# Output weights in two transfers, and sixteen partitions of the last w_down rows loaded halfway through

## The chip, the cores and the metric

The kernel runs on one core of one Trainium2 chip. The metric is the device time of one launch in microseconds; smaller is better. Times named "at 397.69" are counted from the first instruction of the profiled execution.

## The reference

One decoding step of a transformer block with one new token: a pre-norm attention over a long cache, then a pre-norm gated feed-forward part. All tensors are bf16.

```
h  = x + attention(layernorm(x)) @ wo
h2 = h + (gelu(layernorm(h) @ w_gate) * (layernorm(h) @ w_up)) @ w_down
```

x has 1024 elements (D). There are 32 query heads and 4 key/value heads of 128 elements, so 8 query heads share one key/value head. The cache holds 65536 positions: K and V are 64 MB each. wq and wo have 8 MB each (1024 x 4096 and 4096 x 1024), w_gate and w_up 7 MB each (1024 x 3584), w_down 7 MB (3584 x 1024). Every byte is read once, 173 MB in all.

## The kernel before

Everything is built around one stream of loads, issued by SP in the order of use: wq, then K and V in turns, then wo, w_gate, w_up, w_down. The loads go to `ring`, four slots of 4 MB (32 KB in each of 128 partitions). Slots 0 and 1 (keys R0, R1) take V, slots 2 and 3 (R2, R3) take K; afterwards wo has slots 2 and 3, w_gate 0 and 1, w_up 2 and 3, and w_down 0 and 1 again. The last four rows per partition of w_down do not fit and have a place of their own, `w_end` (128 partitions x 4 rows x 1024, 1 MB), into which nothing else is ever loaded.

Attention runs in eight stages `t` (4 key/value heads x 2 halves of the cache), about 38.7 us each. In a stage, VectorE transposes K in four chunks, TensorE makes the scores (`pe_loop`, a hardware loop), VectorE finds a maximum, ScalarE computes the exponentials (`softmax`, eight activations, keys `lp<t>_<r>`), TensorE multiplies them with V into `acc`, and ScalarE copies `acc` out (`acc_copy`). For every stage SP issues one V load and two K loads. A K half waits until the scores that used its slot are done (semaphore `s_qk`, one step per score group, 32 in all); a V load waits until the stage before has finished with V (`s_step`).

The instructions of an engine stand in the order in which the program is written, through a small recorder (`Flow`): `op` and `dma` note each operation with the keys that it reads and writes, and `issue` sends them out with the waits that follow from the keys. `f.dma(engine, ...)` issues a transfer on that engine's queue (SP's and ACT's are used); each transfer adds 16 to a semaphore when it has landed.

wo is one transfer of 8 MB into both slots; it waits for all 32 score groups (`done`). TensorE then multiplies the attention output with it in 64 matmuls, adds x, and the second norm follows. w_gate, w_up and w_down come by one large transfer each, and w_down in four pieces: 16 rows per partition (`wa`, 4 MB, slot 0), 8 rows (`w_body`, 2 MB, slot 1), then the four rows of `w_end` in two transfers of three rows and one row, with semaphores of their own (`end_sem`). These last two are not recorded by `Flow` but written behind it.

The end is written out by hand: four matmuls that keep TensorE awake (`stay_busy`), a wait for `wa`, 32 wide matmuls (`down_wide`), a copy of their sums by ScalarE (`e_sb`), `add_wide`, a wait for `w_body`, 64 small matmuls (`down`), a wait for each of the `w_end` transfers with 24 and 8 matmuls, two casts, and the output transfer of four partitions.

The profile puts nearly all recorded operations down to one line (L105, in `issue`). Lines of their own have the loop (L436 to L471), the `w_end` transfers (L612), and at the end `down` (L621), `stay_busy` (L628), `down_wide` (L636), `add_wide` (L642) and the copy to `e_sb` (L652).

## Time and profile before

| what | value |
|---|---|
| time, median of 3 runs | 409.34 us (409.29 to 409.46) |
| profiled execution, its own time | 409.97 us |
| its span, first to last instruction | 408.3 us |
| TensorE busy, weight loads aside | 226.1 us (55%) |
| VectorE busy | 201.0 us (49%) |
| ScalarE busy | 40.0 us (10%) |
| bytes read from HBM | 173.02 MB, 424 GB/s over the span |
| mean granted TensorE clock | 0.807 |

The profile is of one execution. Its strip cuts the span into 40 equal slices; a digit is a busy share in tenths, 9 for 90% or more. In the list of DMA queues, q1 is SP's and q10 ACT's; q8 and q14 fetch instructions. In the timeline, a row has the start, the time that its instructions take together, engine, line, operation, and in brackets how long the engine was idle before and who released it; PEq is TensorE's own sequencer. In the table of windows, the columns are the window, its length, busy time and number of instructions of PE, PEld, DVE, ACT and POOL, the granted clock, the busy share of the 16 DMA engines and GB/s.

### The profile page before, as it was taken

The numbers are of one execution on the slowest core, as the hardware profiler recorded it, in microseconds if no ns is written. First come the engines' busy times: TensorE is split into PE (matmuls) and PEld (weight loads), VectorE is DVE, ScalarE is ACT, GpSimd is POOL, SyncE is SP. The second block draws the span as 40 slices with busy tenths as digits, with TensorE's granted clock in tenths as the row PEclk, the third lists the DMA queues.
The fourth block names the chain that finished last, engine by engine and source line by source line (L and its number), as shares of the span: only waits on it lengthen the run. The fifth ranks groups of instructions, "written<-read, shape, count | busy, mean of one in ns | idle before, by whom it ended". The sixth has DMA issues, their size and how long they took to land. (4 is left out here: it accounts for less than half of the span.)

```text
span 408.3 us, 3718 instructions
## 1 busy us (share of the span) xinstructions
PE 226.1 (55%) x1557; PEld 100.1 (25%) x1558; DVE 201.0 (49%) x160; ACT 40.0 (10%) x142; POOL 16.6 (4%) x27
## 2 busy tenths in 40 slices
PE   0433855574677468715863685467456746344156
PEld 0111312231232133202321232233132213132122
DVE  2228760894089328734961686089407940121010
ACT  1000003001300120030003000300130013000000
POOL 4210000001000000010000001000000000020000
PEclk9975995899569778978896689589976986686688
DMA  8999999999999999999999999999999999999994
GB/s 360 411 446 425 459 414 424 446 417 444 424 456 424 411 450 462 417 411 427 485 417 411 417 469 405 424 449 424 443 417 462 417 417 469 405 440 445 401 419 193
DMA packets 4814, 173.10 MB, mean 424 GB/s; under 512 B 580, under 2 KB 584, under 8 KB 840
## 3 DMA queue, kind: packets, MB, share of 16 engines
q1 hardware_dynamic: 4760, 173.02, 98.4%
q8 instruction: 4, 0.07, 0.1%
q14 instruction: 2, 0.02, 0.0%
q10 hardware_dynamic: 48, 0.00, 0.0%
HBM read 173.02 MB, written 0.00 MB: 424 GB/s over the span
## 5 line engine op out<-in xcount | busy, mean ns | idle before, releaser
L105 DVE STREAM_TRANSPOSE ktb<-ring 128x4096 f32<-128x4096 f32 x32 | 141.1, 4418 | 74.3 <-DMA ring<-in_A_k_cache_dram 74.3
L450 PE MATMUL bank<-ktb,qs 128*128 128x512 bf16 x512 | 131.7, 416 | 54.4 <-PEq L436 54.4
L450 PEld LDWEIGHTS bank<-ktb,qs 128*128 128x128 bf16 x512 | 51.4, 103 | 131.5 <-issue 85.6
L462 PE MATMUL bank<-ring,pt 128*32 128x512 bf16 x512 | 43.9, 518 | 36.5 <-PEq L436 36.5
L105 ACT ACTIVATE pt<-sc,nb 128x256 bf16<-128x256 f32 x64 | 31.5, 493 | 258.3 <-DVE nb L105 258.3
L105 DVE STREAM_TRANSPOSE sc<-bank 128x512 f32<-128x512 f32 x32 | 22.2, 695 | 38.0 <-PE bank L450 38.0
L462 PEld LDWEIGHTS bank<-ring,pt 128*32 128x32 bf16 x512 | 18.6, 125 | 58.7 <-issue 54.4
L105 PE MATMUL bank<-ring,xz 128*32 128x512 bf16 (+1 forms) x192 | 16.0, 505 | 21.7 <-DMA ring<-in_B_w_up_dram 7.7
L105 DVE STREAM_TRANSPOSE ktb<-bank 128x512 f32<-128x512 f32 (+1 forms) x6 | 4.0, 672 | 32.9 <-PE bank L105 32.6
L105 DVE TENSOR_REDUCE mx<-sc 128x8 f32<-128x2048 f32 x8 | 18.3, 2286 | 0.3
L454 PE MATMUL bank<-ident_f,mx 128*8 128x128 f32 x8 | 2.6, 320 | 25.8 <-PEq L436 25.8
L105 POOL COPY qs<-qsel 128x512 bf16<-128x512 bf16 x4 | 5.3, 1326 | 233.5 <-PE bank L450 219.5
L105 PEld LDWEIGHTS bank<-ring,xz 128*32 128x32 bf16 x192 | 6.4, 125 | 30.0 <-issue 15.6
L105 ACT ACTIVATION_READ_ACCUMULATOR pt<-sc,nb 128x1 f32 x64 | 11.9, 186 | 0.0
L471 PE MATMUL bank<-sel,acc_sb 128*128 128x8 f32 x64 | 8.2, 255 | 6.2 <-PEq L436 6.2
L471 PEld LDWEIGHTS bank<-sel,acc_sb 128*128 128x128 f32 x64 | 7.7, 191 | 10.0 <-issue 10.0
L105 ACT COPY acc_sb<-bank 128x512 f32<-128x512 f32 x8 | 4.7, 586 | 46.5 <-PE bank L462 46.5
L454 PEld LDWEIGHTS bank<-ident_f,mx 128*8 128x8 f32 x8 | 0.7, 83 | 29.5 <-issue 29.5
L105 PE MATMUL bank<-ring,ktb 128*32 128x512 bf16 x64 | 5.2, 492 | 4.7 <-DMA ring<-in_A_wo_dram 4.7
L456 PE MATMUL bank<-diag,ones_f 8*128 8x8 f32 x16 | 3.7, 299 | 5.7 <-PEq L436 5.7
L105 POOL MEMSET ktb<- 128x1024 bf16 (+2 forms) x3 | 3.5, 1164 | 76.6 <-PE bank L450 76.6
L105 DVE TENSOR_TENSOR h_col<-bank,x_col 128x8 f32<-128x8 f32 x1 | 0.2, 166 | 12.3 <-PE bank L105 12.3
(97 smaller groups left out, 60.9 us busy)
## 6 DMA issues: line engine op xcount, KB each, us to landing
ring<-in_A_k_cache_dram SPq DMA_DIRECT2D x16, 4096.0 KB, 25.1
ring<-in_A_wq_dram SPq DMA_DIRECT2D x2, 4096.0 KB, 16.6
ring<-in_B_w_gate_dram SPq DMA_DIRECT2D x1, 7168.0 KB, 26.1
ring<-in_B_w_up_dram SPq DMA_DIRECT2D x1, 7168.0 KB, 28.9
ring<-in_B_w_down_dram SPq DMA_DIRECT2D x1, 4096.0 KB, 22.0
ring<-in_B_w_down_dram SPq DMA_DIRECT2D x1, 2048.0 KB, 26.5
w_end<-in_B_w_down_dram SPq DMA_DIRECT2D x1, 768.0 KB, 27.7
w_end<-in_B_w_down_dram SPq DMA_DIRECT2D x1, 256.0 KB, 10.5
```

The source lines that it names most:

```text
L105: ins = getattr(self.eng[e], o["call"])(**o["kw"])
L450: m = nc.tensor.matmul(bank[c][:], lhsT=qs[:, jt].rearrange("p s c -> p (s c)")[:, s * P:(s + 1) * P], rhs=mv[:, :, J, :, u], start=(s == ...
L454: nc.tensor.transpose(out=mxT_ps, in_=mx1[:], identity=ident_f[:]).then_inc(s_step, 1)
L456: nc.tensor.matmul(bc_ps, lhsT=ones_f[0:rep, :], rhs=diag[:], start=True, stop=True).then_inc(s_step, 1)
L462: m = nc.tensor.matmul(acc[32 * q:32 * q + 32, :], lhsT=pt[:, c, n, :, :].rearrange("p h s -> p (h s)"), rhs=v_sb[:, c, :, n, :], start=(c ...
L471: m = nc.tensor.matmul(o_ps, lhsT=acc_sb[:, u * Dh:(u + 1) * Dh], rhs=sel[:, u:SQ:NS], start=(u == 0), stop=(u == NS - 1))
```

## The change

There are two parts.

First, wo comes in two transfers of 4 MB, by heads 0 to 15 and 16 to 31 of each partition's rows. The first goes into slot 2 and waits for 30 of the 32 score groups, those that read slot 2; the second goes into slot 3 and waits for all 32. The matmuls read the key of their own half.

Second, the four `w_end` rows of the last 16 partitions (112 to 127) are loaded by five transfers of 5, 4, 3, 2 and 2 partitions, issued on ACT's queue behind `acc_copy(3)`, which is half way through the eight stages. Each moves 8 KB per partition. They share the semaphore of the load of x. The two `w_end` transfers at the end now move 112 partitions. TensorE waits for the five early transfers together with `w_body`, ahead of the 64 matmuls of `down`. In the order of SP's instructions, the first `w_end` transfer now stands behind the barrier at the end of the recorded part, where it stood ahead of it.

```diff
+    x_sem = tc.alloc_semaphore("x_landed")
...
+    FA = CW // D
+    FB = FC - FA
+    wb_src = B_w_down[P * FA:F, :].rearrange("(p e) n -> p e n", p=P)
+    early = [5, 4, 3, 2, 2]
+    PE0 = P - sum(early)
+
+    def early_rows():
+        p0 = PE0
+        for n in early:
+            at = f.dma("act", w_end[p0:p0 + n, :, :], wb_src[p0:p0 + n, FB - FZ:FB, :], r=["lp3_0"], sem=x_sem)
+            p0 += n
+        return at
...
         if t + 1 < NT2:
             acc_copy(t)
+        if t == 3:
+            early_at = early_rows()
...
-    f.dma("sp", wv, A_wo.rearrange("(p c) n -> p c n", p=P), w=["R2", "R3"], wait=done, sem=r_sem[2])
+    wo_v = A_wo.rearrange("(p c) n -> p c n", p=P)
+    HC = Hq // 2
+    f.dma("sp", wv[:, 0:HC, :], wo_v[:, 0:HC, :], w=["R2"], wait=[(s_qk, NT2 * CPH - DCH)], sem=r_sem[1])
+    f.dma("sp", wv[:, HC:Hq, :], wo_v[:, HC:Hq, :], w=["R3"], wait=done, sem=r_sem[2])
...
-            op("pe", "matmul", r=["o2z", "R2", "R3"], w=["B6"], ...
+            op("pe", "matmul", r=["o2z", "R%d" % (2 + c // HC)], w=["B6"], ...
...
-        d = nc.sync.dma_start(out=w_end[:, e1 - FB + FZ:e2 - FB + FZ, :], in_=wb_src[:, e1:e2, :])
+        d = nc.sync.dma_start(out=w_end[0:PE0, e1 - FB + FZ:e2 - FB + FZ, :], in_=wb_src[0:PE0, e1:e2, :])
...
+        nc.tensor.wait_ge(x_sem, early_at)
         nc.tensor.wait_ge(sem2, at2)
```

More of the change, by code (lines that the diff above doesn't have):

```diff
@@ L220 @@
     x_in = sb("x_in", [XU, XV, DC], BF16)
+    x_sem = tc.alloc_semaphore("x_landed")
     ones_f = sb("ones_f", [P, P])
     op("dve", "memset", w=["ones_f"], ap=ones_f[:], constant=1.0)
-    f.dma("act", x_in[:], A_x[0, 0].rearrange("(u v j) -> u v j", u=XU, j=DC), w=["x_in"], r=["ones_f"], sem=tc.alloc_semaphore("x_landed"))
+    f.dma("act", x_in[:], A_x[0, 0].rearrange("(u v j) -> u v j", u=XU, j=DC), w=["x_in"], r=["ones_f"], sem=x_sem)
     wq_tiles = []
@@ L415, in acc_copy @@
         op("act", "copy", wait=[(s_step, STEPS * t + 4)], inc=(from_act, 1), out=acc_sb[:], in_=acc[:])
+    FA = CW // D
[3 more added lines that the diff above has]
+    PE0 = P - sum(early)
+    assert PE0 % 16 == 0
+    def early_rows():
[4 more added lines that the diff above has]
+        return at
     for t in range(NT2):
@@ L519 @@
     op("pool", "tensor_copy", r=["o2_bf"], w=["o2z"], out=o2z[:, :, 0], in_=o2_bf[:])
-    FA = CW // D
-    FB = FC - FA
     at_ps = bank[6][:]
     wv = slot(2, 2).rearrange("p (c n) -> p c n", c=Hq)
-    f.dma("sp", wv, A_wo.rearrange("(p c) n -> p c n", p=P), w=["R2", "R3"], wait=done, sem=r_sem[2])
+    wo_v = A_wo.rearrange("(p c) n -> p c n", p=P)
+    HC = Hq // 2
+    f.dma("sp", wv[:, 0:HC, :], wo_v[:, 0:HC, :], w=["R2"], wait=[(s_qk, NT2 * CPH - DCH)], sem=r_sem[1])
+    f.dma("sp", wv[:, HC:Hq, :], wo_v[:, HC:Hq, :], w=["R3"], wait=done, sem=r_sem[2])
     for c in range(Hq):
@@ L529 @@
             q = 2 * (c % 2) + s
-            op("pe", "matmul", r=["o2z", "R2", "R3"], w=["B6"], out=at_ps[32 * q:32 * q + 32, :], lhsT=o2z[:, c, :],
+            op("pe", "matmul", r=["o2z", "R%d" % (2 + c // HC)], w=["B6"], out=at_ps[32 * q:32 * q + 32, :], lhsT=o2z[:, c, :],
                rhs=wv[:, c, :].rearrange("k (p s c) -> k s p c", s=DS, c=C4)[:, s], start=(c < 2), stop=(c >= Hq - 2), tile_position=(0, 32 * q))
@@ L600 @@
     wb = slot(1)[:, 0:FB * D].rearrange("p (e n) -> p e n", e=FB)
-    wb_src = B_w_down[P * FA:F, :].rearrange("(p e) n -> p e n", p=P)
     parts = [(wa, 0, FA, f.dma("sp", wa, B_w_down[0:P * FA, :].rearrange("(p e) n -> p e n", p=P), after=["R0"], inc=(r_sem[0], 16)), r_sem[0])]
```

## The prediction

> **What bounds the kernel now.** I began with the page's strip of the span and its table of DMA queues.

> ```profile
> DMA  8999999999999999999999999999999999999994
> ...
> q1 hardware_dynamic: 4760, 173.02, 98.4%
> q8 instruction: 4, 0.07, 0.1%
> q14 instruction: 2, 0.02, 0.0%
> q10 hardware_dynamic: 48, 0.00, 0.0%
> ```

> From the second slice to the last but one the 16 DMA engines are never free: SP's queue (q1) fills 98.4% of their time. No computing engine is near that (PE 55%, DVE 49%). So bytes set the time, and a byte moved to an earlier place finds no hole to fall into. Each stream is cut by partitions, 8 to an engine, and the packet records give 65536 bytes in 2.42 us: 27.05 bytes/ns for one engine, 433 GB/s for 16.

> Then the end, in the timeline: what waits last for those bytes?

> ```profile
> 397.69 3.54 PE L636 MATMUL bank<-ring,ktb 128*32 128x512 bf16 x32 [1.51 <-DMA ring<-in_B_w_down_dram]
> ...
> 401.43 0.59 ACT L652 COPY e_sb<-bank 128x512 f32<-128x512 f32 x1 [23.59 <-PEq L647]
> ...
> 402.18 0.66 PE L642 MATMUL bank<-e_sb,fold 128*64 128x128 f32 x8
> ...
> 403.79 1.08 PE L621 MATMUL bank<-ring,ktb 128*32 128x128 bf16 x64 [0.94 <-PEq L655]
> ...
> 405.07 0.63 PE L621 MATMUL bank<-w_end,ktb 128*32 128x128 bf16 x32 [0.21 <-PEq L655]
> ```

> PE stands still until the first 4 MB of w_down (`wa`) have landed, at 397.65 on the slowest engine. From there a fixed string runs for 8 us: matmuls, a copy, `add_wide`, branches, the last matmuls to 405.70, then casts and the output to 408.25. The later pieces are nearly due: 2 MB of w_down are in at 402.57, the two `w_end` transfers at 404.40 and 405.03, against uses at 403.78, 405.04 and 405.35. So there are two nearly equal ends, `wa` on the slowest engine and, 0.3 us behind, `w_end` on the slowest engine.

> Last, how far apart the engines are. Near the end, windows of the stream show it (last two columns: busy share of the 16, GB/s).

> ```profile
> 402.50:403.00 0.50, 0.34 (x8) 0.10 (x2) 0.00 (x0) 0.00 (x0) 0.00 (x0) 1.00 0.49 193
> 403.00:403.50 0.50, 0.00 (x0) 0.00 (x0) 0.00 (x0) 0.00 (x0) 0.00 (x0) 1.00 0.28 111
> 403.50:404.00 0.50, 0.21 (x16) 0.22 (x20) 0.00 (x0) 0.00 (x0) 0.00 (x0) 1.00 0.17 66
> 404.00:404.35 0.35, 0.35 (x40) 0.35 (x32) 0.00 (x0) 0.00 (x0) 0.00 (x0) 1.00 0.08 29
> ```

> At 27 GB/s an engine, some four are at work after 403, two and a half after 403.5, one after 404. By the landing records of `wa` the 16 engines stand 0, .01, .04, .18, .18, .25, .28, .32, .36, .5, .7, .7, 1.36, 1.45, 1.83 and 2.27 us behind the first. The four laggards have a cause: an instruction fetch (q8, q14) broke into their stream at 33.0, 99.7, 145.4, 358.5 and 376.6. Twelve engines are idle while the last finishes. The numbers of the engines are not in the trace.

> **The change, part by part.**

> wo in two. The second half keeps its moment (330.12); the first may go when 30 of 32 score groups are done, at 319.8 by PE's row. Today wo is issued only 1.7 us before the first engine has finished V (331.8), and three engines show a first wo packet 0.4 to 0.9 us longer than 2.42. That returns to leading engines, not to the last one. It costs one more issue on SP (0.33 us) with a 4 MB backlog behind it. PE can do half of its 5.2 us of wo matmuls before 353.7, so `w_up` is issued some 2.6 us before 359.03; its bytes are not due until 368.2 and PE next waits for `w_gate` (371.1). Worth 0.

> The wait on `x_landed`. It stands in front of 64 matmuls on PE's tail, its data 200 us old. The event instructions there follow each other at 0.106 us, so +0.1.

> `w_end` by 112 partitions. Seven partitions in place of eight: 8 KB less per engine, 8192/27.05 = 0.30 us earlier. In the new order SP's first `w_end` issue falls behind the barrier that ends at 394.4 (before: 376.74). The 2 MB ahead of it keep the first engine busy to 399.8, which covers that by 5 us. Since PE's string is the later end, the gain is at most 0.3 and I count 0.

> The five early transfers. ACT issues them after `acc_copy(3)`, at 188.7; five issues of 0.33 us end by 190.5, and ACT's next work is the exponentials at 217.0, so nobody queued behind them on ACT notices. The weight is in where they go. The output transfer has 4 partitions and leaves as 4 packets on 4 engines at once; `x_in`, 32 partitions, as 32 packets with 16 completions. So a transfer of n partitions uses n engines, one partition each, and I take the same first ones each time (of 4 engines, 3 are those of the transfer of 3, and so on). Then the loads are 5, 5, 3, 2 and 1 packets of 8 KB on five engines, in a stream without holes. They stand *ahead of* `wa`, while what they relieve stands behind it.

> What does one such packet cost its engine? Low end: its bytes, 0.30 us. High end: the two 8 KB instruction packets, which also come from another queue into the full stream. They took 0.32 and 0.34 us, and the stream's next 32 KB packet behind them 1.87 and 1.56 in place of 1.21: 0.98 and 0.69 lost each. On the other side stands `x_in`: its packets on ACT's queue alternated with the stream's at 1.216 us and delayed nothing, but they have 64 bytes. I take 0.69, the lower of the two rows of equal size; the ends are 0.30 and 0.98 (below nothing it cannot be: the bytes must move).

> Sum: 5 x 0.69 = 3.45 on two engines. If they are of the middle of the field (0.34 behind the first), they stand at 3.79, and `wa` completes 3.79 - 2.27 = 1.5 us later. All behind it shifts with it. With 0.1 for the wait: +1.6. The profiled execution is 409.97 (408.25 and 1.72 around it) and would be 411.5; the three timed runs lie 0.63 lower, so **410.9**.

> The same at K and V: engines 3 us late delay each score stage by as much, but V is issued 8 us and `w_gate` 6 us before the stream runs dry, so no hole opens.

> [...]

> **Rivals.**

> *Only bytes count (not slower).* A packet costs 0.30: 1.51 on two engines, from 0.34 to 1.85, still ahead of the last engine at 2.27. `wa` is where it was, the time 409.34 + 0.1, or down to 409.0 where `w_end` is the last end and gets its 0.3. It decides while a packet costs under (2.27 - 0.34)/5 = 0.39. For: `x_in`'s even alternation. Against: both 8 KB rows.

> [...]

> *A laggard is among the five.* Nothing says the five engines are leaders. If the last engine is one with five packets, it pays 1.5 to 3.4 in full: 410.9 to 412.9. By chance alone 2 in 16, and as much again for the third laggard.

> *The slowest engine loses its bad luck (faster).* It took two fetches, 0.69 at 145.4 and 1.43 at 358.5. With more instructions on ACT and PE, one may hit another engine; then the field ends at 1.83, 0.44 sooner, with the 0.3 of `w_end` 408.7. Only a shift of both makes it over 0.2%.

> *It does not do what it says.* Were small transfers not split, one engine would take 16 packets: 4.8 to 11 us late, 412 or more. The output's four packets speak against it.

> **How the numbers follow.** Packets at about 0.69: 0.34. Only bytes: 0.31. Colliding destinations: 0.18. A laggard hit: 0.08. Better luck: 0.06. No split: 0.03. A measurement of this kernel tells about 0.2%, 0.8 us. Slower by more are the first (but for 0.03, packets near 0.5), the third, fourth and sixth: 0.60. Within are the second and that 0.03: 0.34. Faster: 0.06. The forecast's own range, 0.55 to 0.98 a packet, is 410.2 to 412.4. The whole range goes from 409.0 (only bytes, with the 0.3) to 412.6 (high packets, part of the laggard case) and leaves out the luck case and the worst of the collisions.

> **What would show it.** Right: PE's wait ahead of the wide matmuls (`wa`) ends near 399.2 in place of 397.69, with two engines at work alone in the last windows of the stream, and q10's 16 packets of 8 KB near 190 to 205 followed by longer stream packets. [...] Only bytes: they take 0.30, the stream's next packet 1.21 or 2.42, and 397.69 stays. Wrong altogether: idle gaps in the DMA strip around wo or the end, or a `wa` that lands before 397.

## The result, and the profile after

The changed kernel takes 413.88 us (413.32 to 413.95), against 409.36 in the same runs before: 1.0102 of it (95% interval 1.009 to 1.0113), or +4.5 us. The prediction had the direction, but 410.9 and a range that ended at 412.6.

Of the page's parts, the strip of the DMA engines and the list of queues answer to the first lines shown of before.

```profile
DMA  8999989998999899999999999999999999999993
...
q1 hardware_dynamic: 4872, 172.89, 98.1%
q10 hardware_dynamic: 80, 0.13, 0.1%
q8 instruction: 4, 0.07, 0.1%
q14 instruction: 2, 0.02, 0.0%
```

The bytes are the same, and so is the share of time in which the engines count as busy. ACT's queue has 0.13 MB more, SP's as much less. Hardly anything idles; yet the span is 412.2 in place of 408.3. So the same bytes were busy for longer.

The end of the timeline shows where that is paid (start, time together, operation, idle time before it and its releaser).

```profile
399.50 3.42 PE L653 MATMUL bank<-ring,ktb 128*32 128x512 bf16 x32 [1.33 <-DMA ring<-in_B_w_down_dram]
...
403.13 0.58 ACT L669 COPY e_sb<-bank 128x512 f32<-128x512 f32 x1 [23.33 <-PEq L664]
...
403.89 0.66 PE L659 MATMUL bank<-e_sb,fold 128*64 128x128 f32 x8
...
406.56 1.90 PE L638 MATMUL bank<-ring,ktb 128*32 128x128 bf16 x64 [2.01 <-DMA ring<-in_B_w_down_dram]
...
408.66 1.05 PE L638 MATMUL bank<-w_end,ktb 128*32 128x128 bf16 x32 [0.20 <-PEq L672]
```

Four amounts make the difference up. The wide matmuls start at 399.50, 1.81 after the 397.69 of before: `wa` is late. The 64 matmuls of `w_body` start at 406.56 in place of 403.79, so 2.77 late: 0.96 more, and now a transfer releases them, where before only the branch did. They then take 1.90 in place of 1.08, and the last 32 take 1.05 in place of 0.63. 1.81 + 0.96 + 0.82 + 0.42 = 4.0, the profiled execution's whole loss (413.95 against 409.97).

Windows of the last stretch show the other half of the story (last three columns: granted TensorE clock, busy share of the 16 DMA engines, GB/s).

```profile
402.50:403.00 0.50, 0.42 (x4) 0.00 (x0) 0.00 (x0) 0.00 (x0) 0.00 (x0) 0.50 1.02 229
403.00:403.50 0.50, 0.35 (x2) 0.22 (x3) 0.00 (x0) 0.37 (x1) 0.00 (x0) 0.85 0.92 205
...
405.00:405.50 0.50, 0.00 (x0) 0.00 (x0) 0.00 (x0) 0.00 (x0) 0.00 (x0) 1.00 0.45 94
...
407.00:407.50 0.50, 0.50 (x30) 0.50 (x24) 0.00 (x0) 0.00 (x0) 0.00 (x0) 0.50 0.22 86
```

At 402.5 all 16 engines are busy and move 229 GB/s, about half of what 16 busy engines moved before (433 with large packets; at 402.5 before it was 193 at a share of 0.49, which is 394 for a full share). This is not a tail of a few laggards; it is a crowd at half speed. In the packet records, 16 KB packets of `w_body` that took 0.61 us take up to 1.22, and 6 KB packets of `w_end` 0.35 on the mean in place of 0.24. The last of the rows shows the late matmuls at a granted clock of 0.50. Before, they ran at 1.00. What the slower matmuls add (0.82 and 0.42) belongs to the profiled execution and is not shown to come from the change: in the profiles of all twelve runs below, the 64 matmuls took 1.08 again, even where PE had waited longer for `w_body` (2.52 us with the cut alone, against 2.01 here).

I use one measure below: the *lost stream time*, the sum over SP's packets of their duration less their bytes at 27.02 bytes/ns, over all 16 engines. Between 192 and 220 us, where the early packets run, it is 0.0 us before and 17.2 after. From 396 to the end it is 3.4 before and 30.7 after. The early packets themselves took 0.31 to 0.35 us each, hardly more than their bytes. So the loss is not in the packets that were added but in those beside them. The landing records agree: the V load of stage 4 lands 1.41 us later on the mean of the 16 engines, 22.6 us of engine time, which is nearly 17.2 and 16 x 0.31 of early packets. Even the first engine lands 0.66 later.

### The profile page after: what moved, and what is told of

It reads as the page before. It is cut to its first block, busy times and chain, and to the rows that moved or that the text cites. A ratio compares the mean times of both kernels' runs of the same rounds, so it can differ in the third digit from the quotient of the medians.

```text
span 412.2 us, 3726 instructions
## 1 busy us (share of the span) xinstructions
PE 226.8 (55%) x1558; PEld 100.6 (24%) x1558; DVE 201.0 (49%) x160; ACT 40.0 (10%) x142; POOL 16.6 (4%) x27
## 3 DMA queue, kind: packets, MB, share of 16 engines
q1 hardware_dynamic: 4872, 172.89, 98.1%
HBM read 173.02 MB, written 0.00 MB: 420 GB/s over the span
## 5 line engine op out<-in xcount | busy, mean ns | idle before, releaser
L479 PEld LDWEIGHTS bank<-ring,pt 128*32 128x32 bf16 x512 | 18.4, 125 | 58.4 <-issue 54.0
```

The lines of the kernel that those rows point to most:

```text
L479: m = nc.tensor.matmul(acc[32 * q:32 * q + 32, :], lhsT=pt[:, c, n, :, :].rearrange("p h s -> p (h s)"), rhs=v_sb[:, c, :, n, :], start=(c ...
```

## Experiments

### The wo split alone

```diff
-        if t == 3:
-            early_at = early_rows()
...
-        d = nc.sync.dma_start(out=w_end[0:PE0, ...], in_=wb_src[0:PE0, e1:e2, :])
+        d = nc.sync.dma_start(out=w_end[:, ...], in_=wb_src[:, e1:e2, :])
```

(PE's wait for the early transfers goes with them, and SP issues the first `w_end` transfer ahead of the barrier again, at 377.10.)

> wo in two transfers stays, the early transfers and the cut to 112 partitions are taken back. Both theories of the early part say 409.3 to 409.4, the time of before, PE's wait for wa ending near 397.7 and the w_down pieces landing as before (402.6, 404.4, 405.0). If the wo split itself costs something (a third theory: its extra transfer and wait move later loads), this run shows it alone: 410 or more.

409.46 us, 0.9996 (0.9984 to 1.0009). The split costs nothing and brings nothing. The long first packets of wo are gone (lost stream time from 330 to 340 us: 1.5 before, 0.4 here), on engines that do not set the end.

### Early transfers with a whole w_end

```diff
-        d = nc.sync.dma_start(out=w_end[0:PE0, ...], in_=wb_src[0:PE0, e1:e2, :])
+        d = nc.sync.dma_start(out=w_end[:, ...], in_=wb_src[:, e1:e2, :])
```

(In this run, and in all below that write the early rows a second time at the end, SP waits for the early transfers before it issues `w_body`. They have landed over 160 us before that.)

> The five early transfers stay as they are, but the two w_end transfers at the end load all 128 partitions again (the 16 early partitions are read twice, 128 KB more, 0.3 us per engine). Theory A, wrong destinations (an engine that writes into partitions which are another engine's share of the stream hinders both; it costs twice, at 190 us and again at the end through the cut by 112): the first half of the loss stays, wa lands near 399.4, but w_body follows 5 us behind it with the same spread, near 404.5 in place of 406.4, and the stream packets of the end keep their 0.61 us for 16 KB; 411.2 to 412.0. Theory B (a packet of another queue costs its engine a fixed 0.7 us wherever it writes, and the cut by 112 is harmless): as the changed kernel plus 0.3, 413.9 to 414.3.

412.02 us, 1.0062 (1.0045 to 1.0078): 0.02 over A's range, and 1.9 us under the changed kernel, where B has it above. `wa` is complete at 399.80, `w_body` 4.89 behind it (402.57 - 397.65 = 4.92 before, 6.97 in the changed kernel). The lost stream time at the end is back at 3.4; in mid-stream it stays, 18.4 us between 190 and 220. So the cut by 112 makes a loss of its own. The new order of SP's instructions is not what makes it: here too the first `w_end` transfer is issued behind the barrier (397.12).

### One even early transfer, with the cut

```diff
-    early = [5, 4, 3, 2, 2]
+    early = [16]
```

> The 16 partitions come early by one transfer of 16 partitions (one packet on each engine) in place of five; the cut to 112 at the end stays. Theory A: the early loss is smaller and even over the engines (wa near 398 to 398.5), but the end still collides: 16 KB packets of w_body near 1.1 us, w_body complete 6 us or more behind wa in place of 4.9; 411 to 412.5. Theory B: one packet of 0.7 us on each engine and nothing at the end: wa near 398.3, 410.0.

412.40 us, 1.0077 (1.006 to 1.0094). Lost stream time 15.0 us in mid-stream and 28.8 at the end, `wa` at 398.76 and `w_body` 6.4 behind. Here the early packets themselves are long too, 0.31 to 0.93 us. Spreading the 16 packets over all engines leaves most of the loss. That speaks against the uneven loading (5, 5, 3, 2, 1) as its cause, and B's 410.0 is out.

### The same packets, to the engines' own share

```diff
-            at = f.dma("act", w_end[p0:p0 + n, :, :], wb_src[p0:p0 + n, FB - FZ:FB, :], ...)
+        for p0, n in ((0, 5), (1, 4), (2, 3), (3, 2), (32, 2)):
+            own = slice(p0, p0 + 4 * n - 3, 4)
+            at = f.dma("act", w_end[own, :, :], wb_src[own, FB - FZ:FB, :], ...)
```

with a whole `w_end` at the end.

> As the run with five early transfers and a whole w_end, with the same number and size of packets on the same engines, but every early packet goes to a partition that I take to be its own engine's share (partitions 0, 4, 8, 12, 16, then 1, 5, 9, 13 and so on, in steps of 4). Theory A: the packets cost their bytes alone, 0.30 us each, no stream packet of another engine grows, the last engine need not be touched: wa between 397.6 and 398.2, 409.4 to 410.2. Theory B: no difference between this run and that one.

409.89 us, 1.0014 (1.0004 to 1.0023), and `wa` at 397.80. Sixteen packets of 8 KB, 5, 5, 3, 2 and 1 on five engines, each 0.31 to 0.32 us, and no stream packet of any engine is longer than 1.23 (32 KB) or 2.43 us (64 KB): the lost stream time from 192 to 220 is -0.1 us. This decides between the theories: number, size, queue and time of the packets are those of the run before last, and only the partition numbers differ, in SBUF and in HBM. That the shares lie in steps of 4 was a supposition of mine; the -0.1 us agrees with it.

### One share further

```diff
-        for p0, n in ((0, 5), (1, 4), (2, 3), (3, 2), (32, 2)):
+        for p0, n in ((4, 5), (5, 4), (6, 3), (7, 2), (36, 2)):
```

> As the run with early packets in the engines' own share, but every partition number is 4 higher, so that each packet goes to the share of the next engine: one foreign writer at a time in a share, where the changed kernel sends up to four into one. Theory A1 (writers of one share divide its rate, nothing else): a packet and the stream packet beside it lose 0.3 us each, some 5 us of stream time over all engines in place of 17, wa 0.3 to 1.2 us later, 409.9 to 410.8. Theory A2 (leaving one's own share costs a fixed time, on all engines): as much as in the run with partitions 112 to 127 and a whole w_end, 17 to 19 us of stream time, 411.7 to 412.4.

412.17 us, 1.0071 (1.0054 to 1.0088). The list of queues for 192 to 216 us, first of the own-share run, then of this one (packets, MB, share of 16 engines' time):

```profile
q1 hardware_dynamic: 216, 10.42, 100.4%
q10 hardware_dynamic: 32, 0.13, 1.3%
```

```profile
q1 hardware_dynamic: 193, 9.90, 99.6%
q10 hardware_dynamic: 32, 0.13, 1.4%
```

ACT's queue does the same in both; SP's is as busy and moves 0.52 MB less. The lost stream time is 16.2 us, a little under A2's 17 to 19 and far over A1's 5: A2, not A1. If the shares lie as the own-share run takes them, with which its -0.1 us agrees, there is one foreign writer at a time in a share here and up to four in the run with partitions 112 to 127 and a whole `w_end`: 16.2 us are lost against 18.4. So it does not take four writers in one share.

### Target or source

The neighbour run moved the place in HBM as well as the place in SBUF. Two runs part them.

```diff
+            to, of = [slice(p0 + d, p0 + d + 4 * n - 3, 4) for d in (0, 4)]   # mirror: (4, 0)
+            at = f.dma("act", w_end[to, :, :], wb_src[of, FB - FZ:FB, :], ...)
```

> Early packets as in the own-share run (targets 0, 4, 8 and so on), but each reads the rows of the partition 4 higher in HBM, as the neighbour run does; the whole w_end load at the end writes the right rows over them. If it is the target in SBUF that decides (theory A2): no lost stream time, as in the own-share run, 409.7 to 410.3. If it is the place in HBM that the packet reads from (theory C: engines collide in memory): 16 us of lost stream time and 411.9 to 412.5, as in the neighbour run.

> The mirror of the last one: early packets read the own partitions' rows in HBM and write the partitions 4 higher. Theory A2: 16 us of lost stream time, 411.9 to 412.5. Theory C: none, 409.7 to 410.3.

With the source moved: 410.04 us, 1.001 (1.0001 to 1.002), lost stream time -0.1. With the target moved: 412.08 us, 1.006 (1.0043 to 1.0076), lost stream time 16.5. It is the target partition.

### How much for how many

```diff
-    early = [5, 4, 3, 2, 2]
+    early = [5]
```

> Only the first early transfer (5 partitions, 112 to 116, 40 KB), and a whole w_end at the end. If every foreign packet costs its own about 1.1 us of stream time: 5 to 6 us over all engines in place of 17 to 19, the last engine of wa 0.3 to 0.9 later than before, 409.5 to 410.4. If the first foreign packet costs most and the rest ride along: 10 us or more, 411 or more.

```diff
-            at = f.dma("act", w_end[p0:p0 + n, :, :], wb_src[p0:p0 + n, FB - FZ:FB, :], ...)
+            at = f.dma("act", w_end[p0:p0 + n, 0:1, :], wb_src[p0:p0 + n, FB - FZ:FB - FZ + 1, :], ...)
```

> All five early transfers to partitions 112 to 127, but one row of the four (2 KB packets, a quarter of the bytes), and a whole w_end at the end. If the loss goes with the bytes that are written to foreign shares: 4 to 5 us of lost stream time, 409.6 to 410.3. If it goes with the number of packets: 15 us or more, 411.5 or more.

Five packets: 410.16 us, 1.0016 (1.0006 to 1.0025), lost stream time 12.2. The two signs disagree: the time fell into the range of "each its own", the lost time into that of "the first costs most". The packet records side with the second. Of the 16 stream packets under way at 195.2 us, one on each engine, every one is too long, by 0.59 to 0.83 us. Together that is 11.2 of the 12.2.

Sixteen packets of a quarter of the size: 409.94 us, 1.0012 (1.0003 to 1.0022), lost stream time 4.0 from 190 to 220, a fifth of the 18.4. So the number of packets does not set the loss, and neither do their bytes alone: a quarter of the bytes lost a fifth, but five of sixteen packets lost two thirds. What arrives at the same moment may be what counts; no run here varies that alone.

### The cut alone

```diff
+    op("dve", "memset", w=["w_end_z"], ap=w_end[96:P, :, :], constant=0.0)
...
-        if t == 3:
-            early_at = early_rows()
```

(PE's wait for the early transfers goes with them, and the `w_body` load waits for the zeros.)

> No early transfers at all; w_end at the end by 112 partitions. The last 16 partitions of the four rows are left out (zeros, set at the start), so 128 KB less are read. Theory A with a loss at the end of its own: wa lands as before (397.5 to 397.8), but w_body comes 6 us or more behind wa in place of 4.9, its 16 KB packets up to 1.1 us, and the whole lies 0.8 to 2.0 us over before: 410.2 to 411.4. If the end collided only because the engines were already spread by the early packets: 409.0 to 409.4.

410.77 us, 1.0036 (1.0022 to 1.005), with 128 KB less to read. Its timeline:

```profile
397.58 2.53 PE L652 MATMUL bank<-ring,ktb 128*32 128x512 bf16 x32
...
404.25 1.08 PE L637 MATMUL bank<-ring,ktb 128*32 128x128 bf16 x64 [2.52 <-DMA ring<-in_B_w_down_dram]
...
405.99 1.04 PE L637 MATMUL bank<-w_end,ktb 128*32 128x128 bf16 x32 [0.66 <-DMA w_end<-in_B_w_down_dram]
```

`wa` is where it was before (397.54), but PE waits 2.52 us for `w_body`, complete at 404.21 in place of 402.57, and then again for `w_end`. Lost stream time from 396 on: 33.2 us, of which 4.4 are in packets of `w_body` and 28.8 in those of `w_end` (before: 0.9 and 2.6). By 112 partitions an engine gets seven partitions in place of eight (in the records of the changed kernel, 112 packets of 6 KB for 16 engines, before 128). The leading engines start on them while the others still write `w_body`: of the 195 packets that start from 401 to 405 us, 191 are under 8 KB, and `w_body` is complete only at 404.21. The cut collides without any early packet. That it does so because engines write other engines' partitions is concluded from the runs on the early packets; no run changes the partitions of the end load alone.

### The other part undone

```diff
-    f.dma("sp", wv[:, 0:HC, :], wo_v[:, 0:HC, :], w=["R2"], wait=[(s_qk, NT2 * CPH - DCH)], sem=r_sem[1])
-    f.dma("sp", wv[:, HC:Hq, :], wo_v[:, HC:Hq, :], w=["R3"], wait=done, sem=r_sem[2])
+    f.dma("sp", wv, wo_v, w=["R2", "R3"], wait=done, sem=r_sem[2])
```

> The changed kernel with wo in one transfer again, issued after the last score group as before. If the wo split plays no part in the loss: 413.3 to 414.2, as the changed kernel. If the split had been needed to keep the stream full now that score groups come 2 us later: wo is issued at 332.3 against a first engine that ends V at 332.6, so leading engines idle for up to 1.5 us; those do not set the end, still under 414.5.

413.43 us, 1.0111 (1.0088 to 1.0134), not to be told from the changed kernel. With score groups 2 us late, lost stream time at wo's seam (330 to 340) is 7.1 us in place of 0.3, and on the mean of the engines `wa` comes 0.8 later (398.18 against 397.42); its last engine comes at 399.68 against 399.46. The loss falls on leaders, as expected.

### The same bytes moved ahead in another cut

```diff
+        at = f.dma("act", w_end[:, FZ - 1, 0:NB], wb_src[:, FB - 1, 0:NB], ...)
...
+        c0 = NB if i else 0
+        d = nc.sync.dma_start(out=w_end[:, ..., c0:D], in_=wb_src[:, e1:e2, c0:D])
```

> The same 128 KB are moved ahead by one early transfer of all 128 partitions, 1 KB each (half of the last row), and the last transfer at the end loads the other half by 128 partitions. Nothing else differs from the changed kernel. Theory A (each engine keeps to its own share): no lost stream time, wa 0.3 us later, the end where it was: 409.3 to 409.9. Theory B' (any packets of ACT's queue in mid-stream cost a fixed time per packet): 8 packets on every engine would cost 5 us or more, 414 and up.

409.87 us, 1.0009 (0.9996 to 1.0021): as before within what is measured. 128 packets of 1 KB on ACT's queue, each near 0.05 us, and 0.3 us of lost stream time. The 0.3 us that A expected on `wa` show on the mean of the engines (396.41 against 396.04 before), not on the last one (397.64 against 397.65). So 128 KB can be moved ahead at no loss, by rows and not by partitions. It gains nothing either: the stream had no hole there, and the last engine of `wa` still sets the end. No version tried here beats the kernel before.

## Why the prediction was wrong

**What bounds the kernel** held: SP's queue fills 98.1% of the engines' time (98.4% before), PE's tail starts with `wa` on the slowest engine, and bytes moved ahead delay `wa` (by 0.37 us on the mean of the engines in the run by rows). The failing is in two terms.

**The step on the cut by 112** failed outright. It reads "8 KB less per engine, 0.30 us earlier ... the gain is at most 0.3 and I count 0". The cut alone costs 1.5 us (1.0036), and between the run with early transfers and a whole `w_end` and the changed kernel lie 1.9. In place of a gain, 33.2 us of stream time are lost at the end, and `w_body` is complete at 404.21 in place of 402.57. I had counted its bytes and kept the rate, without asking which engine writes which partition once there are 112. Without this term the early half (412.02) lies inside the range; with it the time left it.

**The price of an early packet** came out near in size for a wrong reason, which is luck. I took 0.69 from the instruction fetches, a fixed cost on the packet's own engine, and got +1.5 for `wa`; it was +1.81 in the profile. But the own-share run has 0.31 per packet and nothing else. The loss sits in the streams of all engines. Instruction fetches were the wrong row for the price; `x_in`, which I set aside for its 64 bytes, showed what ACT's queue costs.

**The rival of colliding destinations**, at 0.18, named the right cause, the target: with the target moved 16.5 us of stream time are lost, with the source moved none (-0.1). Behind it stood groups of partitions that each take writes at one engine's rate; no run shows that term. What the runs show in its place is larger: by my estimate, a rate shared by the writers would lose 16 x 0.31, about 5 us, in the neighbour run, and 16.2 were measured. The rival bears on the cut by 112 as well, which my sum has at 0: the cut alone lost 33.2 us.

**The clock** was not in the sum: in the profiled execution 0.82 + 0.42 = 1.24 of the 4.0 us come from matmuls at a granted 0.50. I had PE's string as "fixed". In the profiles of the twelve other runs the 64 matmuls took 1.08 each time, and in seven of them the last 32 took 0.63, so this part is not shown to be a price of the change. What `stay_busy` does for the clock is not shown either: every version here has it.

**Rightly at nothing** stood the wo split (0.9996) and the issue of five transfers on ACT. The wait on `x_landed` is hidden behind `w_body` here and has no measured price. That early bytes only cost bytes, the rival at 0.31, is what the own-share run (-0.1 us of lost stream time), the run with the source moved (-0.1) and the run by rows (0.3) show; the runs with packets to other partitions lost 4.0 to 18.4. My list of how far the 16 engines stand behind is off by up to 0.11 against the landing records (the last is at 2.24), which moves nothing.

## What to carry to other kernels

In a load stream that keeps all DMA engines busy, count which engine writes which partitions, not bytes alone: here a last load of 112 partitions in place of 128 lost 33.2 us of stream time in place of 3.4, and 16 packets to partitions 4 higher lost 16.2 in place of -0.1, with the engines still shown as busy (99.6%). By theory A that is because engines were given partitions that others were writing. If a piece of a load has to move, cut it along the rows and leave the partitions whole: by rows, the same 128 KB lost 0.3 us. When a rival prices one half of a change, ask at once whether the other half falls under it too.

## What was not expected of the hardware

Packets sent to other partitions lengthened packets on engines that carried none of them. In the neighbour run all 16 stream packets under way at 194.8 us are too long, by 0.22 to 0.45 us; in the own-share run none from 192 to 220 us is, by more than 0.02. If the shares lie in the steps of 4 that the own-share run takes, the writers are five engines and the owners they disturb five of the first six, yet the first engine to land the next V load comes 0.8 us later than in the own-share run (216.87 against 216.06), the mean 1.0 (217.80 against 216.78). In the changed kernel, joining each packet to the one that starts as it ends gives 16 chains, one for each engine: from 184 to 222 us seven without an early packet lose 0.72 to 0.74 us each, and four more without one 1.5 to 1.8. By the same steps these four may be the owners of partitions 112 to 127; the records have no numbers of engines, so that stays open. The loss is some three times the bytes' own time: 16.2 us of stream time for 16 x 0.31. Why engines with no part in it lose is open; these runs show only that the target partition decides it, not the source and not the number of packets.

Five foreign packets that arrive together lost 12.2 us, two thirds of what sixteen lost. And busy shares hide all of it: 99.6% against 100.4% of the engines' time, with 0.52 MB less moved in 24 us.
